# Interleaving the first attention segment with the linear branch's key and value chunks, with early weights aliased into late feature storage

## The chip, the cores and the metric

The kernel runs on one core of one Trainium2 chip. The metric is the device time of one execution in microseconds (us); the time given for a kernel is the median of its runs. Besides the timed runs there is one profiled execution, whose span runs from its first to its last instruction.

## What is computed

Two attention branches read the same x (2048 rows, width 640, 32 heads of 20), and a sigmoid gate per row mixes them. Branch A is linear attention with softmax feature maps. Branch B cuts the rows into four segments of 512; within a segment it is softmax attention under a causal mask, and a memory carried from segment to segment is mixed in per head.

```python
# A: linear attention
pq, pk = q @ w_phi, k @ w_phi                      # per head, 20 x 20
phi_q = concat(softmax(pq), softmax(-pq)); phi_k = likewise
kv = phi_k^T v;  z = sum_s phi_k                   # over all 2048 rows
a  = ((phi_q kv) / (phi_q z + 1e-6)) @ A_wo
# B: four segments, M = z = 0 before the first
p = softmax(qs ks^T * 20**-0.5 + mask)
o = g * (phi(qs) M / (phi(qs) z + 1e-6)) + (1 - g) * (p vs)
M, z = M + phi(ks)^T vs, z + sum phi(ks)           # phi(t) = t+1 if t>0 else exp(t)
b = o @ B_wo
out = gate * a + (1 - gate) * b                    # gate = sigmoid(x . gate_w)
```

## The kernel before

x is held transposed in SBUF (`xT`, 5 chunks of 128 features by 2048 rows), in quarters loaded by transposing DMAs. PSUM is used as four single banks (`bank`, tag "one") and two double banks (`banks2`, tag "two"). The double banks serve folded weights, key features and attention scores alike.

The program runs in stages, in this order.

1. *Fold.* Key weights are transposed on TensorE (`transposed`, from `WkN` to `WkT`) and multiplied by the feature matrix `Wphi` (`fold_weight`), giving `WkA`.
2. *Linear keys and values.* For each of sixteen chunks of 128 rows, `key` multiplies by `WkA`, takes two exponentials on ScalarE (`Ek`), and on VectorE sums them per head, inverts and multiplies (`ksum`, `krec`, `phk`). `value` multiplies by `WvA` and ScalarE copies the result to `vA`. From chunk 8 on, the query weights are folded into `WqA`, and from chunk 10 on ScalarE permutes the columns of `stq` into `WqB` (L272). The instructions here are mostly placed by the framework's scheduler.
3. *Query projection of segment 0, sums and products.* Five `emit_q` run among 160 tiny matmuls that sum the features (`zb_ps`). VectorE adds them in 32 small steps (L321), and `kv_ps` forms the products (L333).
4. *Gates and pools.* The gates of rows and heads are computed for all rows at once, the pools of the first part are closed, and those of the second part opened.
5. *Segment 0's keys and values* (L664 to L671).
6. *The list.* `ORDER` is a string of letters, each one unit of work, that goes out in just that order; matmuls, ScalarE work and some GpSimd work are pinned to it with `keep_in_program_order`. Eighty P's run through it, five for each pair of head groups.

| letter | unit |
|---|---|
| P | one pair of score tiles: matmuls into both double banks, two exponentials `PT` of 128x1024 on ScalarE (L377), causal selects on GpSimd (L547) |
| V, M | a group's values (40 small matmuls, `nd_ps`) and its memory read and update |
| Y | query features of a group for the memory read |
| k, K | half a chunk of B's keys into `kpads` (two buffers), with a transposing DMA to `kTs` after the second half; and its features `phik` |
| v, w | half a chunk of B's values, evicted by VectorE (v) or ScalarE (w) |
| q, u | one fifth of a segment's queries into `qd` (two buffers), evicted by VectorE (q) or ScalarE (u), and scattered into `qTp` by DMAs on SP's queue |
| f, d, n | branch A's query features, weights and outputs |
| l, o, z | loading a row block transposed, and half of its output projection |
| t, b, p | the start of the tail |

After the list comes a tail: the last values and memory read, and the output projections of the last segment.

All weights are loaded on SP's queue: `WkN` and `WvA` first, then `xT` and `WqT` by transposing DMAs, then `WkB`, `WvB`, `stq`, `WoA`, `WoB` (L89 to L162).

Of the kernel before, what the change touches and what calls it, by code (L numbers as in the profile page):

```python
# [7 lines left out]
ACT = mybir.ActivationFunctionType  # L8
# [7 lines left out]
def kernel(  # L16
# [38 lines left out]
    def banks2(name):  # L55
# [12 lines left out]
    wAs = ExitStack()  # L68
    wA = wAs.enter_context(tc.tile_pool(name="wA", bufs=1, side="right"))
# [4 lines left out]
    wA1 = ExitStack()  # L74
    wk = wA1.enter_context(tc.tile_pool(name="wk", bufs=1, side="right"))
    WkA = wk.tile([P, KC, D], BF16, name="WkA")
    WvA = wk.tile([P, KC, D + 1], BF16, name="WvA")
    Wc = wk.tile([P, KC, DH], BF16, name="Wc")
    WkN = wk.tile([P, KC, D], BF16, name="WkN")
    WkT = wk.tile([P, KC, D], BF16, name="WkT")  # L80
    WqT = wk.tile([P, KC, D], BF16, name="WqT")
    nc.scalar.dma_start(out=Wc, in_=A_w_phi.rearrange("h f g -> (h f) g").rearrange("(c p) g -> p c g", p=P))
    nc.scalar.dma_start(out=WvA[:, :, D:D + 1],
                        in_=gate_w.rearrange("(c p o) -> p c o", p=P, o=1))
    beta_b = const.tile([P, H], BF16, name="beta_b")
    nc.scalar.dma_start(out=beta_b, in_=B_beta.partition_broadcast(P))
    def load_xT(lo, hi):
        nc.sync.dma_start_transpose(out=xT[:, :, lo:hi], in_=x2[lo:hi, :])
    nc.sync.dma_start(out=WkN, in_=A_wqkv[:, D:2 * D].rearrange("(c p) n -> p c n", p=P))  # L89
    nc.sync.dma_start(out=WvA[:, :, 0:D],  # L90
                        in_=A_wqkv[:, 2 * D:3 * D].rearrange("(c p) n -> p c n", p=P))
    load_xT(0, P)
    load_xT(P, L)
    for q4 in range(1, 4):
        load_xT(q4 * L, (q4 + 1) * L)
    nc.sync.dma_start_transpose(out=WqT, in_=A_wqkv[:, 0:D])

    NW = 8
    wz = wk.tile([P, L], BF16, name="wz")
    nc.vector.memset(wz, 0.0)
    wu = bank([P, L], "warm_ps")
    for n in range(WARM):
        m = nc.tensor.matmul(wu, lhsT=wz[:, 0:P], rhs=wz, start=True, stop=True)
        if n:
            tc.keep_in_program_order(m)
    ident_f = wk.tile([P, P], F32, name="ident_f")  # L110
    nc.gpsimd.memset(ident_f, 0.0)
    tc.keep_in_program_order(nc.gpsimd.affine_select(
                            out=ident_f, in_=ident_f, pattern=[[-1, P]],
                            compare_op=ALU.not_equal, fill=1.0, base=0,
                            channel_multiplier=1))
    ident = wk.tile([P, P], BF16, name="ident")
    nc.vector.tensor_copy(out=ident, in_=ident_f)
    for t in qTp:
        nc.vector.memset(t, 0.0)
    hn_f = wk.tile([P, KC, NW], F32, name="hn_f")  # L120
    tc.keep_in_program_order(nc.gpsimd.memset(hn_f, 1.0))
    tc.keep_in_program_order(nc.gpsimd.affine_select(
                            out=hn_f, in_=hn_f, pattern=[[8, KC], [-DH, NW]],
                            compare_op=ALU.is_ge, fill=0.0, base=0, channel_multiplier=1))
    tc.keep_in_program_order(nc.gpsimd.affine_select(
                            out=hn_f, in_=hn_f, pattern=[[-8, KC], [DH, NW]],
                            compare_op=ALU.is_ge, fill=0.0, base=DH - 1, channel_multiplier=-1))
    Wphi = wk.tile([P, KC, NW, DH], BF16, name="Wphi")
    tc.keep_in_program_order(nc.vector.tensor_tensor(
        out=Wphi, in0=Wc[:, :, None, :].to_broadcast([P, KC, NW, DH]),  # L130
        in1=hn_f[:, :, :, None].to_broadcast([P, KC, NW, DH]), op=ALU.mult))
    blk = wk.tile([P, KC, NW // 2], F32, name="blk")
    tc.keep_in_program_order(nc.gpsimd.memset(blk, 1.0))
    nc.gpsimd.affine_select(out=blk, in_=blk, pattern=[[8, KC], [-2 * DH, NW // 2]],
                            compare_op=ALU.is_ge, fill=0.0, base=0, channel_multiplier=1)
    nc.gpsimd.affine_select(out=blk, in_=blk, pattern=[[-8, KC], [2 * DH, NW // 2]],
                            compare_op=ALU.is_ge, fill=0.0, base=2 * DH - 1,
                            channel_multiplier=-1)
    bd01 = const.tile([P, 4], F32, name="bd01")
    tc.keep_in_program_order(nc.gpsimd.memset(bd01, 1.0))  # L140
    nc.gpsimd.affine_select(out=bd01, in_=bd01, pattern=[[-32, 4]],
                            compare_op=ALU.is_ge, fill=0.0, base=0,
                            channel_multiplier=1)
    nc.gpsimd.affine_select(out=bd01, in_=bd01, pattern=[[32, 4]],
                            compare_op=ALU.is_ge, fill=0.0, base=31,
                            channel_multiplier=-1)
    for t in (kpads[:, :, :, DH:32], Msb):
        tc.keep_in_program_order(nc.gpsimd.memset(t, 0.0))


# [4 lines left out]
    WoA = wB.tile([P, KC, D], BF16, name="WoA")  # L155
    WoB = wB.tile([P, KC, D], BF16, name="WoB")
    stq = wk.tile([P, KC, D], BF16, name="stq")
    nc.sync.dma_start(out=WkB, in_=B_wk.rearrange("(c p) n -> p c n", p=P))
    nc.sync.dma_start(out=WvB, in_=B_wv.rearrange("(c p) n -> p c n", p=P))
    nc.sync.dma_start(out=stq, in_=B_wq.rearrange("(c p) n -> p c n", p=P))  # L160
    nc.sync.dma_start(out=WoA, in_=A_wo.rearrange("(c p) n -> p c n", p=P))
    nc.sync.dma_start(out=WoB, in_=B_wo.rearrange("(c p) n -> p c n", p=P))  # L162
# [12 lines left out]
    def transposed(ic):  # L175

        tp = ps.tile([P, KC, P], BF16, name="tp_ps", tag="one", bufs=4)
        for c in range(KC):
            tc.keep_in_program_order(nc.tensor.transpose(
                out=tp[:, c, :], in_=WkN[:, ic, c * P:(c + 1) * P], identity=ident))  # L180
        tc.keep_in_program_order((nc.scalar.copy if ic % 2 == 0 else nc.vector.tensor_copy)(
            out=WkT[:, :, ic * P:(ic + 1) * P], in_=tp))

    def fold_weight(dst, WT, ics=range(KC), pinned=False):
        for ic in ics:
            if pinned:
                for n in ((0, 1, 2) if ic == 0 else (ic + 2,) if ic + 2 < KC else ()):
                    transposed(n)
            fp = banks2("fold_ps")
            for n, w in enumerate(WIN):  # L190
                c, lo, hi = w
                bk = lo // 16
                m = nc.tensor.matmul(fp[:, bk, (lo - 16 * bk) * DH:(hi - 16 * bk) * DH],
# [3 lines left out]
                if pinned and n == 0:  # L197
                    tc.keep_in_program_order(m)
# [660 lines left out]
```

## Time and profile before

| | us |
|---|---|
| median of 3 runs | 328.86 (328.55 to 328.91) |
| span of the profiled execution | 326.7 |
| first exponential of a score | 95.21 |
| end of the last exponential of a score | 310.87 |

The profiled execution's own time isn't given apart from its span; the median of the runs lies 2.2 us above it.

| engine | busy us | share of the span | instructions |
|---|---|---|---|
| TensorE (PE) | 306.2 | 94% | 3915 |
| VectorE (DVE) | 237.6 | 73% | 587 |
| ScalarE (ACT) | 256.2 | 78% | 370 |
| GpSimd (POOL) | 167.5 | 51% | 357 |

Busy time counts an instruction from its start to its end; where matmuls overlap in the array, TensorE counts as busy throughout, so its share isn't the share of its peak. PEld is the weight load of TensorE, which overlaps the matmuls. "SPq" and "ACTq" are the DMA-issuing queues of SyncE and ScalarE. In a group's line, "out<-in" names the tiles, then come the shapes and the count, the busy us and the mean ns of one, and the idle time before them with what ended it.

### The profile page before, as it was taken

The page shows a single profiled execution, that of the slowest core. Times are in us where ns is not written, and L with a number is a line of the kernel's source. Part 1 is how long each engine was busy: PE and PEld are TensorE (multiplying, and loading weights), DVE is VectorE, ACT ScalarE, POOL GpSimd, SP SyncE. Part 2 cuts the span into 40 slices and gives each one's busy share as a digit, 9 for nine tenths or more (in the row PEclk, how much of TensorE's full clock was granted, in tenths as well). Part 3 has the DMA queues.
Part 4 walks back from the last instruction along what each step waited for, and adds up shares of the span by engine and source line. Part 5 has one row for each costly group of instructions (what it writes and reads, how often), then busy time and mean ns, then how long its engine had stood idle before and what let it go on. Part 6 is the DMA issues. An engine that isn't in the chain of part 4 may idle for free.

```text
span 326.7 us, 9643 instructions
## 1 busy us (share of the span) xinstructions
PE 306.2 (94%) x3915; PEld 200.6 (61%) x3915; DVE 237.6 (73%) x587; ACT 256.2 (78%) x370; POOL 167.5 (51%) x357
## 2 busy tenths in 40 slices
PE   8899999999898999889999999999999898999994
PEld 4677766698554566555655666566566555666673
DVE  6599997757752577945879999397879956669622
ACT  3677899610479899999999989998888799978811
POOL 4000000002214557987566999675789676668930
PEclk9999999999999999999999999999999999989999
DMA  7999600020232021514121320442303142225252
GB/s 209 175 212 318 220 2 0 25 59 2 64 74 57 20 51 50 74 22 94 34 59 46 72 57 23 53 97 50 90 22 68 42 64 63 62 62 69 48 108 80
DMA packets 63147, 24.50 MB, mean 75 GB/s; under 512 B 54016, under 2 KB 63104, under 8 KB 63104
## 3 DMA queue, kind: packets, MB, share of 16 engines
q1 hardware_dynamic: 61360, 23.54, 32.1%
q8 instruction: 30, 0.49, 0.6%
q10 hardware_dynamic: 1744, 0.36, 0.5%
q14 instruction: 13, 0.11, 0.1%
HBM read 5.77 MB, written 2.62 MB: 26 GB/s over the span
## 4 chain that ended last, share of the span: by engine, by line
PE 59%; DVE 15%; ACT 11%; POOL 9%; issue 3%; DMA 2%; ACTq 0%; DVEq 0%
PE o_ps L374 10%; PE proj L374 7%; ACT PT L377 7%; PE nd_ps L374 7%; PE q_ps L280 6%; PE k_ps L229 6%; PE st_ps L374 6%; PE v_ps L217 6%; PE pf_ps L374 5%; POOL PT L547 4%; POOL oA L471 3%; DVE t L466 2%; PE kv_ps L333 2%; DMA Wc<-in_A_w_phi_dram 2%; PE mem_ps L374 1%
## 5 line engine op out<-in xcount | busy, mean ns | idle before, releaser
L377 ACT ACTIVATE PT<-st_ps 128x1024 bf16<-128x1024 f32 x160 | 155.8, 1037 | 11.2 <-PE st_ps L374 9.3
L547 POOL TENSOR_SCALAR_AFFINE_SELECT PT<-PT 128x256 bf16<-128x256 bf16 (+1 forms) x224 | 96.4, 450 | 55.7 <-ACT PT L377 54.1
L374 PE MATMUL st_ps<-qTp,kTs 32*128 32x384 bf16 (+3 forms) x512 | 41.7, 301 | 6.3 <-ACT PT L377 6.2
L374 PEld LDWEIGHTS <-PT 128*128 128x128 bf16 x1280 | 36.3, 96 | 7.3 <-issue 2.7
L374 PE MATMUL nd_ps<-vB,PT 128*128 128x32 bf16 x1280 | 39.3, 177 | 1.3 <-POOL PT L547 0.6
L390 POOL MEMSET vB<- 128x16 bf16 x4 | 0.5, 116 | 75.3 <-PE kv_ps L333 75.3
L374 PEld LDWEIGHTS <-xT 128*128 128x128 bf16 x320 | 28.8, 97 | 16.4 <-issue 5.7
L374 PEld LDWEIGHTS <-kTs 32*128 32x128 bf16 (+1 forms) x552 | 16.6, 92 | 32.1 <-issue 27.1
L466 DVE TENSOR_TENSOR t<-num_ps,dd 128x320 f32<-128x320 f32 x64 | 29.0, 481 | 4.6 <-PE num_ps L374 3.8
L471 POOL TENSOR_TENSOR oA<-t,t 128x320 bf16<-128x320 f32 x32 | 27.7, 867 | 4.2 <-DVE t L466 4.0
L374 PEld LDWEIGHTS <-oT 128*128 128x128 bf16 x240 | 22.5, 99 | 11.2 <-issue 2.1
L236 ACT ACTIVATE Ek<-k_ps 128x640 bf16<-128x640 f32 x32 | 21.8, 768 | 8.2 <-ACT vA L222 4.7
L374 PE MATMUL proj<-WvB,xT 128*128 128x320 bf16 x160 | 27.2, 299 | 0.3 <-ACT vB L380 0.3
L374 PE MATMUL proj<-WkB,xT 128*128 128x320 bf16 x160 | 26.4, 299 | 1.2 <-DVE kpads L485 0.6
L241 DVE TENSOR_REDUCE ksum<-Ek 128x64 f32<-128x1280 bf16 x16 | 23.7, 1480 | 5.0 <-ACT Ek L236 5.0
L618 POOL TENSOR_TENSOR oB<-td,tm 128x320 bf16<-128x320 f32 (+2 forms) x25 | 22.0, 881 | 8.0 <-DVE tm L609 8.0
L229 PE MATMUL k_ps<-WkA,xT 128*128 128x320 bf16 x160 | 24.3, 299 | 1.6 <-ACT Ek L236 1.3
L280 PE MATMUL q_ps<-xT,WqB 128*128 128x512 bf16 x100 | 25.3, 380 | 0.2 <-DVE mtmp L623 0.2
L374 PE MATMUL pf_ps<-xT,WqA 128*128 128x512 bf16 x100 | 24.8, 380 | 0.0
L217 PE MATMUL v_ps<-WvA,xT 128*128 128x320 bf16 (+1 forms) x160 | 24.5, 300 | 0.0
L485 DVE CAST kpads<-proj 128x320 bf16<-128x320 f32 x32 | 15.3, 484 | 9.9 <-PE proj L374 9.8
L577 DVE RECIPROCAL rden<-nd_ps 128x16 f32<-128x16 f32 x32 | 8.0, 250 | 20.0 <-PE nd_ps L374 19.7
(114 smaller groups left out, 533.7 us busy)
## 6 DMA issues: line engine op xcount, KB each, us to landing
out_dram<-osb SPq DMA_DIRECT2D x12, 160.0 KB
qTp<-qd SPq DMA_DIRECT2D x8, 128.0 KB
WkN<-in_A_wqkv_dram SPq DMA_DIRECT2D x1, 800.0 KB
WvA<-in_A_wqkv_dram SPq DMA_DIRECT2D x1, 800.0 KB
WkB<-in_B_wk_dram SPq DMA_DIRECT2D x1, 800.0 KB
WvB<-in_B_wv_dram SPq DMA_DIRECT2D x1, 800.0 KB
stq<-in_B_wq_dram SPq DMA_DIRECT2D x1, 800.0 KB
WoA<-in_A_wo_dram SPq DMA_DIRECT2D x1, 800.0 KB
```

Source lines behind the costliest of these rows:

```text
L217: m = nc.tensor.matmul(vp[:, 0:n], lhsT=xT[:, c, sc * P:(sc + 1) * P], rhs=WvA[:, c, half * 320:half * 320 + n], start=(c == 0), stop=(c = ...
L229: m = nc.tensor.matmul(kp[:, half, 0:320], lhsT=xT[:, c, sc * P:(sc + 1) * P], rhs=WkA[:, c, half * 320:(half + 1) * 320], start=(c == 0), ...
L236: nc.scalar.activation(out=Ek[:, sgn, :].rearrange("p (a n) -> p a n", a=2), in_=kp[:, :, 0:320], func=ACT.Exp, scale=1.0 if sgn == 0 else ...
L241: nc.vector.tensor_reduce(out=ksum, in_=Ekv.rearrange("p b f i -> p b i f"), axis=AX.X, op=ALU.add)
L280: nc.tensor.matmul(q_ps, lhsT=WqB[:, cc, c * P:(c + 1) * P], rhs=xT[:, cc, s * L:(s + 1) * L], start=(cc == 0), stop=(cc == KC - 1))
L374: return kept(nc.tensor.matmul(*a, **k))
L377: return kept(nc.scalar.activation(**k))
L466: nc.vector.tensor_tensor(out=tt, in0=nm.rearrange("p (h d) -> p h d", d=DH), in1=Lin.cs[:, t, sgn, 16 * bk_:16 * bk_ + 16, None].to_broad ...
L471: tc.keep_in_program_order(nc.gpsimd.tensor_tensor(out=seg.oA[:, t, bk_ * 320:(bk_ + 1) * 320], in0=ts_[0].rearrange("p h d -> p (h d)"), ...
L485: nc.vector.tensor_copy(out=kp[:, half * 16:(half + 1) * 16, 0:DH], in_=pp.rearrange("p (h d) -> p h d", d=DH))
L547: nc.gpsimd.affine_select(out=v, in_=v, pattern=[[0, n], [1, P]], compare_op=ALU.is_ge, fill=0.0, base=0, channel_multiplier=-1)
L618: tc.keep_in_program_order(nc.gpsimd.tensor_tensor(out=o[:, :, at:at + n1 - n0], in0=td2[:, :, n0:n1], in1=tm2[:, :, n0:n1], op=ALU.add))
```

## The change

Segment 0's projections go first. The fold, the linear keys and values, the sums and products become letters of the list too, and the first attention segment's scores run among them. The list is written anew as one string.

| new letter | unit |
|---|---|
| A, B | `key` and `value` of one chunk of the linear branch |
| S, X | the feature sums of one sign, one product |
| T, F, W | a transposition, a fold into `WkA`, a fold into `WqA` |
| L, D, E | a quarter of `xT`, `WqT`, the rest of the loads |
| I, H, J, G | `Wphi`, the masks, the head gate, the row gate of one segment |
| Z | zeroing of `qTp[1]` |
| R | `second_half`: closes the first part's pools, opens the second's, loads `WoA` and `WoB` |

The letters k, K, v, w, q, u and f now count from segment 0.

```diff
-    nc.sync.dma_start(out=WkN, in_=A_wqkv[:, D:2 * D].rearrange("(c p) n -> p c n", p=P))
-    nc.sync.dma_start(out=WvA[:, :, 0:D],
-                        in_=A_wqkv[:, 2 * D:3 * D].rearrange("(c p) n -> p c n", p=P))
...
+    late = phk.rearrange("p c s n -> p (c s n)")[:, 16 * D:32 * D]
+    WkN = late[:, 0:KC * D].rearrange("p (c n) -> p c n", c=KC)
+    WkT = late[:, KC * D:2 * KC * D].rearrange("p (c n) -> p c n", c=KC)
+    Wphi = late[:, 2 * KC * D:2 * KC * D + KC * 8 * DH].rearrange("p (c h g) -> p c h g", c=KC, g=DH)
+    stq = vA[:, 5:10, :]
+    WqT = vA[:, 10:15, :]
+    wz = vA[:, 15, 0:L]
+    WkA = qTp[1].rearrange("p g l -> p (g l)")[:, 0:KC * D].rearrange("p (c n) -> p c n", c=KC)
...
+    load_xT(0, P)
+    load_xT(P, L)
+    for out_, in_ in ((WkB, rows5(B_wk)),
+                      (WkN, rows5(A_wqkv[:, D:2 * D])),
+                      (Wc, rows5(A_w_phi.rearrange("h f g -> (h f) g"))),
+                      (WvB, rows5(B_wv)),
+                      (stq, rows5(B_wq))):
+        kept(nc.scalar.dma_start(out=out_, in_=in_))
...
+    for c in range(KC):
+        kept(nc.gpsimd.tensor_copy(out=WqB[:, c, :].rearrange("p (r g) -> p r g", g=G),
+                                   in_=stq[:, c, :].rearrange("p (g r) -> p r g", g=G)))
...
-            tc.keep_in_program_order(nc.scalar.copy(
-                out=WqB[:, c, :].rearrange("p (r g) -> p r g", g=G),
-                in_=stq[:, c, :].rearrange("p (g r) -> p r g", g=G)))
...
+    def sums(sgn):
+        zb_ps = bank([P, KC, 4 * NCH], "zb_ps")
...
+    def products(n):
+        c, sgn = divmod(n, 2)
+        kv_ps = bank([P, NW, DH], "kv_ps")
...
+    def second_half():
+        a1.close()
...
+        nc.sync.dma_start(out=lt.WoA, in_=rows5(A_wo))
+        nc.sync.dma_start(out=lt.WoB, in_=rows5(B_wo))
...
-    for c in range(4):
-        for half in range(2):
-            emit_k(seg, c, half)
-            emit_v(seg, c, half, scopy)
-        emit_phik(seg, c)
-        if c in (1, 3):
-            lin_features(0, c // 2)
...
+        "kkkkKkkKkkIKKLETTvTFvTFwTFvFwFvuuwvuHJuuLDLABBAA PB PBGAAB PBAWVAB PMBWAWB "
+        "PBAAWVAWB PBAAMB PBAAB PBAVZM P PS PSXXV PXGXMXX PXXXXRG PVGMk Pqq PkV PMqk PuKku "
+        "PVKkkKkk PKMwwYwV Pvvv PMvkfv PfkKf PVkfYYMf Pkkdk PVKYk PvkM PKqK PnVn PMnYlq PVn "
+        "PMYzn Pznq PnvVn PfMf PluvVv PMof PYfwq PVofv PYMdw PlwVYlz PzMYzkn Pzn PknV "
+        "PMnYlkkK PVMKn PYkun Pkon PnV PMKff PVok PYqfM PYlkfYu PvVMlfz PoKd PwV PMuz "
+        "PvYnlwo PVun PMnwYz PVnwM Pno PvnvnY PVn PlMYfo PVf PMff Pofl PYVMd Pz PlnVM PYYzn "
+        "Pon PnV PMnYlz PnVnM PbYz Pnz PV PMpt ")
```

So the early weights share storage with what is written late: `WkN`, `WkT` and `Wphi` lie in the last eight chunks of `phk`, `stq` and `WqT` in chunks 5 to 14 of `vA`, and `WkA` in the query buffer of segments 1 and 3, which Z zeroes after the last A. The five first weights are issued on ScalarE's queue, the transposing DMAs stay on SP's. Two pools hold the segments (`bseg0`, `bseg1`), the second opened at R, and outputs of branch A and weights of the output projection get storage at R. All ScalarE and TensorE work is now pinned to the list.

## Prediction

> **What bounds the kernel now.** First the busy time by stretch. The columns are the stretch (us), its length, then for each engine the busy us and the instructions, the granted clock, and the DMA share and rate.
>
> ```profile
> 0.00:11.50 11.50, 8.76 (x69) 5.04 (x70) 7.78 (x13) 5.41 (x9) 3.48 (x17) 1.00 0.85 203
> 11.50:58.50 47.00, 45.69 (x351) 33.04 (x351) 41.51 (x62) 38.80 (x76) 0.00 (x0) 1.00 0.58 148
> 58.50:80.00 21.50, 21.30 (x349) 17.75 (x348) 14.42 (x57) 5.75 (x12) 0.12 (x2) 1.00 0.12 33
> 80.00:95.20 15.20, 14.27 (x99) 9.04 (x97) 10.57 (x23) 7.79 (x16) 3.80 (x5) 1.00 0.31 70
> 95.20:203.00 107.80, 101.62 (x1465) 61.76 (x1463) 79.37 (x207) 100.83 (x131) 78.00 (x168) 1.00 0.23 51
> 203.00:311.00 108.00, 103.04 (x1474) 65.64 (x1471) 80.43 (x217) 95.84 (x125) 79.72 (x164) 0.98 0.32 61
> 311.00:326.70 15.70, 11.55 (x121) 8.29 (x118) 3.51 (x11) 1.80 (x5) 2.39 (x4) 0.96 0.35 89
> ```
>
> The 80 score steps fill 95.2 to 311, with ACT busy 196.7 of 215.8 us. From 58.5 to 95.2 ACT has 13.5 of 36.7 us of work, and POOL none before 80. So the exponentials come in one dense block behind a stretch that has almost none. PE looks full everywhere, but its matmuls overlap in the records. The chain that ended last has the true pace (start us, us, what):
>
> ```profile
> 11.52 1.52 PE k_ps L229 x10
> 13.03 1.37 PE v_ps L217 x10
> 67.09 0.99 PE zb_ps L312 x40
> 74.07 5.71 PE kv_ps L333 x80
> 93.12 1.09 PE pf_ps L374 x5
> 104.66 1.01 PE nd_ps L374 x40
> ```
>
> That is 0.137 us for a 320-column matmul (299 ns in the groups), 0.22 for 512 columns and 0.025 for the smallest. At these paces all of PE's work is about 266 us: 80% of the score stage, but about 97% of 11.5 to 58.5 (16 chunks of 2.73 and five folds, 45.5 of 47.0). So PE sets the first stage, closely followed by DVE, and ACT the second. The costliest groups give prices (busy over count):
>
> ```profile
> L377 ACT ACTIVATE PT<-st_ps 128x1024 bf16<-128x1024 f32 x160 | 155.8, 1037 | 11.2 <-PE st_ps L374 9.3
> L236 ACT ACTIVATE Ek<-k_ps 128x640 bf16<-128x640 f32 x32 | 21.8, 768 | 8.2 <-ACT vA L222 4.7
> L241 DVE TENSOR_REDUCE ksum<-Ek 128x64 f32<-128x1280 bf16 x16 | 23.7, 1480 | 5.0 <-ACT Ek L236 5.0
> ```
>
> One P, two exponentials, costs ACT 1.95 us. A key chunk A costs ACT 1.36, PE 1.36 and DVE 2.86 (1.48 + 0.55 + 0.83).
>
> **The method and its test.** For each five P with what the list puts between them I add up each engine's work and take the largest. For before the sixteen maxima are 13.8, 11.9, 12.0, 13.0, 14.4, 14.8, 13.0, 14.0, 14.2, 15.3, 11.8, 14.3, 13.3, 14.4, 12.3 and 11.5, together 214.0; the stage took 215.8, a factor of 1.008. ACT is the largest in most. The factor is so near 1 because the prices carry some slack (an exponential that follows another starts 0.92 us after it, not 0.97).
>
> **The change, part by part.**
>
> *Start to first score.* Removed from the head: WkA's fold as the first work. Added: eight k, six to eight v and five q before any A. The first k needs WkB and xT. WkB is now the first weight in its queue, as WkN was before, which released PE at 6.06, so k starts near 6.3. Eight k take 8 x 0.68 = 5.4. Each pair sends a kTs transpose (SP busy 1.23 us, plus landing), and the two kpads buffers let chunk 2 be evicted only when chunk 0's transpose has landed: about 2 us late. Five T, five F and six v are 7.3 us of PE, and the copies between them are the chain that before took from 6.07 to 12.3. That puts q at about 22.
>
> The q need all of WqB. Its source is the fifth weight; 3.3 MB and 0.65 MB of xT at 209 to 318 GB/s (the page's slices) land at 14 to 20. Then POOL makes five strided copies that ACT made in 1.65 each. The trace has no such copy on POOL: from below by the 128x768 memset, 0.74 x 640/768 = 0.6; from above by the 128x84 cast, 0.27 x 640/84 = 2.1. I take 1.3, nearer the middle because the cast is mostly fixed cost: 6.5 us in all, so q starts at 22 to 27, I take 22.5. Five q then go at the pace of their DMAs:
>
> ```profile
> ACT qd L284 <- DMA qTp<-qd: 5.4, 3, 2.0
> ```
>
> Two qd buffers made ACT wait up to 2.0 us; before, the first eviction to the last took 8.7 us (60.72 to 69.42). Before, PE ran sums meanwhile. Now ACT's queue behind the waiting eviction is Ek of the first A, and DVE and the first P wait for that. Then three A and two B precede the first PT: 3 x 1.36 + 4 x 0.42 = 5.8 of ACT. Sum: 22.5 + 1.5 + 8.7 + 0.6 + 5.8 = 39. Ends: 36 if the q DMAs hide behind the copies, 46 if POOL's copies cost 2.1 and kTs lands late in the weight traffic.
>
> *First 15 P (segment 0's attention among A, B, W, S, X).* Added to the A/B stretch: 30 exponentials (29.2 us of ACT), 42 selects on POOL. Per engine (PE, ACT, DVE): P0-P4 28.2, 33.3, 27.0; P5-P9 18.0, 20.7, 18.6; P10 to the point R 14.9, 6.0, 12.6; R to P14 4.4, 4.3, 4.3. Maxima 33.3 + 20.7 + 14.9 + 4.4 = 73.3, times 1.008 = 73.9; I take 73, since before's 11.5 to 58.5 ran PE and DVE both about full with no slip. W (1.0 of ACT each) is in it; WqB's 8.2 us have left ACT. The sums S and the 32 adds behind them (5.9 of DVE) lie under X. Ends: 68 (PE alone 65.5 plus 4%) and 80 (sum plus 10%).
>
> *The other 65 P.* Maxima 16.0, 17.4, 15.3, 13.6, 16.2, 13.9, 13.3, 16.2, 14.4, 13.3, 15.3, 12.8, 11.3 = 189.0, times 1.008 = 190.5. Four stretches now have PE at the top or beside ACT (16.2 to 15.9, 13.9 to 13.8, 16.2 to 16.1, 16.4 to 17.4), and PE's price has no slack in it. Before's stretch with all engines equal (P50, 11.8) took 14.2. I add 2.5: 193, with ends 185 and 203.
>
> *Moved at no cost.* WoA and WoB are loaded at R: SP's queue holds their issue until the last X, and behind it wait the q of segment 1; the first output projection comes some eighteen P later. xT's later quarters and WqT are issued behind the kTs and qTp DMAs, and W0 needs WqT some 10 us after its issue; without that cover W0 holds both fold and key buffers for about 5. The late aliases are reused only after their last reader in the list. The zeroing of qTp[1] (1.76 of DVE) lies in P7, where DVE has 5 against ACT's 4. Evictions shift slightly: 13 instead of 19 vB and 12 instead of 8 qd on ACT, less than 1 us net.
>
> *Tail:* the same work, 15.7.
>
> **Sum:** 39 + 73 + 193 + 15.7 = 320.7, against the profiled 326.7. The median of the runs, 328.86, lies 2.2 above the span, so 322.9; I say **322.5**.
>
> **A rule against it.** DVE's phk multiply (both inputs in SBUF) never ran beside POOL: it took 824 to 826 ns. The like operation that does run beside POOL is spread wide:
>
> ```profile
> L526 DVE TENSOR_TENSOR phiq<-uq,eq x24: 411/678/1083, 137.5 to 298.3; 128x512 bf16<-128x512 bf16 x24
> ```
>
> Thirteen phk will now run beside selects, so by this row each loses 0.27 (median over minimum) to 0.67 us (maximum over minimum): 3.5 to 8.7 in all. The Trainium skill, SBUF — State Buffer, "Who interferes with whom", says that VectorE and GpSimd take a shared port pair by an exclusive lock for a whole instruction; the spread agrees with it, though it doesn't prove it. P0-P9 have DVE at 45.6 against ACT's 54.0, so 8.4 us of cover: I add nothing, and it is a rival.
>
> **The rivals.**
>
> 1. *Two-bank chain* (slower). Key chunks, folds and scores share two double banks. PE can't fill an A until an exponential has drained one, and 1.36 us of filling is longer than one exponential (0.97). If ACT idles for a whole fill at each of thirteen A, 13 x 1.36 = 17.7: 340. It decides the sign from 6.4/13 = 0.5 us each. For it: ACT's longest idle in the first stage, Ek waiting for k_ps (2.8 us over 3 times). Against: B's evictions lie between, and in before's score stage PE waited only 6.2 us for ACT in 80 P.
>
> 2. *Late start.* The first PT at 47 instead of 39 (WqB late, q DMAs unhidden): 330.5, no gain. For it: q's wait above; against: the DMA was idle from 41 to 57, so weights aren't short of bandwidth.
>
> 3. *Port lock decides.* All of 8.7 on the path: 331. Against: the cover.
>
> 4. *Better packed.* First 15 P at 68, the rest at 185, start at 37: 305.7 span, 308. For it: before's first stage ran PE near 97%. Against: ACT held only 91% over before's score stage.
>
> 5. *It doesn't interleave.* The built instruction order has A and B among the scores on PE and ACT, and the same 3915 matmuls; I leave it out.
>
> **How the numbers follow.** Chances: forecast 0.52 (own range 315 to 328), two-bank chain 0.18, late start 0.10, port lock 0.06, better packed 0.14. Faster by over 0.2% (what a measurement here can tell): 0.50 + 0.14 + 0.04 from an incomplete late start = 0.68; within 0.2%: 0.03; slower 0.29. The range 311 to 337 leaves out the lower part of the packed case and the upper end of the chain.
>
> **What would show it.** First PT near 39 (36 to 46); P15's PT near 112; the last PT near 305; the tail at 15.7. ACT idle in 39 to 95 under 10% with the releaser not k_ps. The wait of qd for qTp near 5 us. phk's spread above 826 ns but DVE not ahead of ACT in P0-P9. It would be wrong if ACT is idle over 6 us on k_ps in P0-P8, if the first PT comes after 46, or if the 65 later P take more than 200.

## The result, and the profile after

The changed kernel took 340.76 us (median of 4 runs, 338.86 to 342.15), beside 328.88 us (328.55 to 329.03) for the kernel before on the same chip: a ratio of 1.0365, with a 95% interval of 1.032 to 1.0409. The forecast was 322.5 with a range of 311 to 337, so both the sign and the range were wrong. The profiled execution has a span of 337.1 us (its run took 338.86), where the forecast's sum was 320.7. One run of the experiments' last batch, 340.25 us, stood 1.9% above the fastest of its kernel and is left out there.

Busy time by stretch, cut at the first and every later P that the forecast's terms name (columns as in the prediction's table: stretch, length, then busy us and instructions of PE, PEld, DVE, ACT and POOL, the granted clock, and the DMA's share and rate):

```profile
0.00:47.06 47.06, 34.63 (x226) 20.98 (x227) 24.10 (x48) 17.59 (x32) 12.16 (x25) 0.93 0.67 167
47.06:79.11 32.05, 31.24 (x319) 21.29 (x319) 26.08 (x45) 29.36 (x56) 8.61 (x16) 1.00 0.26 47
79.11:101.23 22.12, 20.62 (x264) 14.12 (x264) 20.10 (x33) 19.33 (x31) 8.44 (x16) 0.91 0.01 2
101.23:123.81 22.58, 22.58 (x376) 19.40 (x376) 14.87 (x67) 9.97 (x14) 9.48 (x24) 0.87 0.18 58
123.81:220.54 96.73, 93.31 (x1257) 59.03 (x1257) 72.57 (x196) 83.22 (x114) 62.51 (x131) 0.98 0.36 68
220.54:321.60 101.06, 96.59 (x1379) 61.95 (x1378) 74.11 (x203) 89.33 (x119) 76.51 (x149) 0.97 0.35 59
321.60:337.10 15.50, 11.19 (x104) 8.03 (x104) 3.52 (x11) 1.60 (x4) 2.45 (x4) 0.96 0.30 80
```

The first three rows after the head are P0 to P4, P5 to P9 and P10 to P14. Set against the sum:

| term | forecast | measured | over by |
|---|---|---|---|
| first P starts | 39 | 47.06 | 8.1 |
| first 15 P | 73 | 76.75 | 3.75 |
| other 65 P | 193 | 197.8 | 4.8 |
| tail | 15.7 | 15.5 | -0.2 |
| span | 320.7 | 337.1 | 16.4 |

The head isn't that steady. Four later kernels leave it as it is here and change only what follows; in their profiles the first P stood at 49.77, 48.77, 48.85 and 48.55. So 47.06 is an early one, and a shift of the first P by less than some 2.7 us in a single profile tells nothing.

Two observations stand in these rows. ACT, which held 91% of the score stage before, holds 231.2 of 274.5 us now, 84%. And the clock column isn't 1.00: in the score stage the granted clock is at half from 97.0 to 107.2 and for 3.4 us each at 168.7, 291.6 and 305.3, 20.5 us in all. The kernel before had 3.4 us of it there. The changed kernel's four runs had a mean clock of 0.954 to 0.970, the kernel before 0.993 in its profile.

The costliest exponentials, and what ACT waited for from the first P to 124 us and from there to 322 us (us in total, times, longest):

```profile
L108 ACT ACTIVATE PT<-st_ps 128x1024 bf16<-128x1024 f32 x160 | 156.2, 1039 | 32.7 <-PE st_ps L105 29.8
```

```profile
ACT PT L108 <- PE st_ps L105: 14.0, 6, 5.8
...
ACT Ek L108 <- PE k_ps L105: 0.2, 1, 0.2
```

```profile
ACT PT L108 <- PE st_ps L105: 16.4, 26, 1.6
```

The exponential costs the same as before (1039 against 1037 ns), but ACT now waits 29.8 us in front of it for the scores, where it waited 9.3. The key features (Ek) hardly wait for the matmul engine: 0.2 us.

The head, on the matmul engine, on POOL and on DVE (start us, us, engine, line, operation, count, and in brackets the idle time before and what ended it):

```profile
7.24 1.53 PE L105 MATMUL proj<-WkB,xT 128*128 128x320 bf16 x10 [1.02 <-DMA xT<-in_A_x_dram]
14.52 6.20 PE L105 MATMUL proj<-WkB,xT 128*128 128x320 bf16 x30 [5.74 <-DMA xT<-in_A_x_dram]
23.00 0.84 PE L194 MATMUL tp_ps<-ident,phk 128*128 128x128 bf16 x10 [2.29 <-DVE kpads L477]
```

```profile
15.02 6.95 POOL L176 COPY WqB<-vA 128x640 bf16<-128x640 bf16 x5 [8.86 <-DMA vA<-in_B_wq_dram]
```

```profile
16.07 0.49 DVE L477 CAST kpads<-proj 128x320 bf16<-128x320 f32 x1 [6.41 <-PE proj L105]
16.48 1.39 DVE L150 CAST ident<-ident_f 128x128 bf16<-128x128 f32 x1
...
18.38 0.95 DVE L491 TENSOR_SCALAR uk<-kpads 128x640 bf16<-128x640 bf16 x1
19.25 1.41 DVE L256 TENSOR_TENSOR hm<-blk,par 128x40 bf16<-128x40 f32 x1
```

Only two of the eight k ran near 7 us (five matmuls each). The other six waited until 14.52 for the second piece of xT, which shared the DMA engines with weights not needed yet: from 9 to 13 us they moved some 245 packets of 256 bytes per us for xT and some 240 of 1280 bytes for the weights, one for one, so 0.06 MB per us for what was waited for and 0.31 for what was not. Then POOL's five copies (1.39 us each) held DVE's small operations: the cast of the identity took 1.39 us here and 0.21 where POOL was idle (shown in the first experiment). The queries started at 31.72 instead of 22.5.

### The profile page after: what moved, and what is told of

The parts are those of the page before. It is cut to its first block, busy times and chain, and to the rows that moved or that the text cites. A ratio compares the mean times of both kernels' runs of the same rounds, so it can differ in the third digit from the quotient of the medians.

```text
span 337.1 us, 9662 instructions
## 1 busy us (share of the span) xinstructions
PE 310.2 (92%) x3915; PEld 204.8 (61%) x3915; DVE 235.3 (70%) x598; ACT 250.4 (74%) x367; POOL 180.2 (53%) x362
## 4 chain that ended last, share of the span: by engine, by line
PE 50%; DVE 11%; ACT 10%; POOL 5%; issue 4%; ACTq 0%; DVEq 0%
PE o_ps L105 9%; PE proj L105 6%; PE nd_ps L105 6%; PE st_ps L105 5%; ACT PT L108 5%; PE q_ps L105 4%; PE pf_ps L105 4%; PE kv_ps L105 4%; PE k_ps L105 3%; POOL PT L539 3%; PE v_ps L105 3%; PE mem_ps L105 2%; ACT ET L108 2%; PE num_ps L105 2%; ACT WqA L111 1%
## 5 line engine op out<-in xcount | busy, mean ns | idle before, releaser
L108 ACT ACTIVATE PT<-st_ps 128x1024 bf16<-128x1024 f32 x160 | 156.2, 1039 | 32.7 <-PE st_ps L105 29.8
L539 POOL TENSOR_SCALAR_AFFINE_SELECT PT<-PT 128x256 bf16<-128x256 bf16 (+1 forms) x224 | 100.4, 467 | 114.4 <-ACT PT L108 112.3
L105 PEld LDWEIGHTS <-xT 128*128 128x128 bf16 x640 | 60.1, 99 | 37.8 <-DMA xT<-in_A_x_dram 7.6
L105 PEld LDWEIGHTS <-kTs 32*128 32x128 bf16 (+1 forms) x552 | 15.8, 92 | 30.6 <-issue 25.8
L105 PE MATMUL proj<-WkB,xT 128*128 128x320 bf16 x160 | 27.2, 316 | 6.9 <-DMA xT<-in_A_x_dram 6.8
L105 PE MATMUL proj<-WvB,xT 128*128 128x320 bf16 x160 | 26.4, 299 | 1.0 <-DVE mtmp L615 0.6
L477 DVE CAST kpads<-proj 128x320 bf16<-128x320 f32 x32 | 15.0, 480 | 15.9 <-PE proj L105 15.9
L105 PE MATMUL q_ps<-xT,WqB 128*128 128x512 bf16 x100 | 24.4, 382 | 0.4 <-DVE kpads L477 0.4
L105 PE MATMUL k_ps<-qTp,xT 128*128 128x320 bf16 x160 | 23.5, 299 | 0.2
L108 ACT ACTIVATE ET<-pf_ps 128x512 bf16<-128x512 f32 x40 | 21.9, 634 | 2.4 <-PE pf_ps L105 2.4
L108 ACT ACTIVATE Ek<-k_ps 128x640 bf16<-128x640 f32 x32 | 20.8, 706 | 3.3 <-ACT WqA L111 1.9
L105 PE MATMUL o_ps<-WoA,oT 128*128 128x320 bf16 x120 | 21.6, 313 | 0.3 <-DVE t L458 0.3
```

Of the source, the lines that this page charges most:

```text
L105: return kept(nc.tensor.matmul(*a, **k))
L108: return kept(nc.scalar.activation(**k))
L477: nc.vector.tensor_copy(out=kp[:, half * 16:(half + 1) * 16, 0:DH], in_=pp.rearrange("p (h d) -> p h d", d=DH))
L539: nc.gpsimd.affine_select(out=v, in_=v, pattern=[[0, n], [1, P]], compare_op=ALU.is_ge, fill=0.0, base=0, channel_multiplier=-1)
```

## The experiments

The first batch took the head and the clock one by one and together; the second combined what the first had taught; the third measured what an extra us of one engine costs; the last asked whether the head and the uneven stretches can be mended. The kernel before had medians of 328.56, 328.59, 328.43 and 328.22 us beside them.

### x first

The four weights after WkB are issued behind a tiny copy on ACT's queue that waits for xT's second piece.

```diff
+    kept(nc.scalar.dma_start(out=WkB, in_=rows5(B_wk)))
+    landed = const.tile([P, 1], BF16, name="landed")
+    scopy(out=landed, in_=xT[:, 0, L - 1:L])
+    for out_, in_ in ((WkN, rows5(A_wqkv[:, D:2 * D])),
...
```

> The changed kernel, but on ScalarE's queue only WkB is issued at once; the four other early weights (WkN, Wc, WvB, stq) wait until the second piece of xT has landed. Theory (queues share by packets: xT's 256-byte packets got 240 per us beside 240 of the weights' 1280-byte packets, and the third k waited for xT until 14.52): the third k starts near 9, TensorE's clock doesn't fall at 11.7 to 18.5, the first PT comes at 38 to 41 instead of 47.06, and the time falls by 5 to 8 us to 333 to 336. Rival (the start is set by the lock between GpSimd's WqB copies and VectorE, or by the q DMAs): the third k comes early all the same, but the first PT stays within 2 us of 47 and the time at 339 to 342.

Measured 345.0 us, ratio 1.0517 (1.0454 to 1.058). The k ran from 7.00 to 12.6 us, as the theory said, but the first P came at 52.2, later than before. DVE in that head:

```profile
9.73 0.21 DVE L152 CAST ident<-ident_f 128x128 bf16<-128x128 f32 x1
...
17.62 0.89 DVE L479 CAST kpads<-proj 128x320 bf16<-128x320 f32 x2 [5.82 <-DMA kTs<-kpads]
...
21.62 0.89 DVE L479 CAST kpads<-proj 128x320 bf16<-128x320 f32 x2 [2.71 <-DMA kTs<-kpads]
...
23.59 3.00 DVE L493 TENSOR_SCALAR uk<-kpads 128x640 bf16<-128x640 bf16 x2
26.51 3.33 DVE L496 TENSOR_TENSOR phik<-uk,ek 128x640 bf16<-128x640 bf16 x2
```

The delayed weights now share the DMA engines with the transposes into kTs, so the evictions wait for those (8.5 us in two waits), and the copies on POOL, now from 21.40 to 29.48, hold uk and phik. The waiting had moved, not gone. The P stretches were as in the changed kernel (32.05, 22.13, 22.66 and 16.90 against 32.05, 22.12, 22.57 and 17.07, and 197.7 against 197.8 for the last 65 P): a later head shifts the rest and nothing else.

### Masks early

The identity, mask and head-mask copies are pinned early on DVE, and so are segment 0's evictions into kpads.

```diff
-        nc.vector.tensor_copy(out=kp[:, half * 16:(half + 1) * 16, 0:DH],
-                              in_=pp.rearrange("p (h d) -> p h d", d=DH))
+        first(nc.vector.tensor_copy(out=kp[:, half * 16:(half + 1) * 16, 0:DH],
+                              in_=pp.rearrange("p (h d) -> p h d", d=DH)), seg.s)
```

> The changed kernel, but VectorE's identity, masks and their copies are pinned ahead of the first evictions of k, so that they don't run while GpSimd permutes WqB (15.02 to 21.97, in which these small steps took 1.2 to 1.4 us each instead of 0.16 to 0.28). Theory (the lock with GpSimd delays the kpads evictions): the fifth k is evicted near 18.5 instead of 22.47, the first PT comes 3 to 4 us earlier, and the time falls by 3 to 4. Rival (the eviction waits for the kTs transpose anyway): first PT within 1 us of 47.06 and no change of time.

Measured 339.95 us, ratio 1.0351 (1.0324 to 1.0378), first P at 47.6: no gain. Another operation meets POOL's copies in their place:

```profile
18.45 2.75 DVE L491 TENSOR_SCALAR uk<-kpads 128x640 bf16<-128x640 bf16 x2
21.12 1.45 DVE L292 CAST CM<-bd 128x32 bf16<-128x32 f32 x1
```

### Sums mixed with products

Each S also issues two of the products X, so that matmuls of 4 and of 160 columns alternate.

```diff
+            for sg, kv_ps in enumerate(kvs):
+                mm(kv_ps, lhsT=phk[:, sc, sg, sgn * P:(sgn + 1) * P],
+                   rhs=vA[:, sc, 6 * sgn * DH:(6 * sgn + NW) * DH],
+                   start=(sc == 0), stop=(sc == NCH - 1))
```

> The changed kernel, but each of the two sums S is issued with two of the products X between its matmuls (4 or 5 narrow ones, then 2 of 160 columns); the same matmuls in all. Theory (narrow matmuls alone let the granted clock fall to half at 97.0 to 107.3): the clock stays full there, or falls for 3.4 us at most, the ten P from P5 to P15 take 41 to 42 instead of 44.7 us, and the time falls by 2 to 4. Rival (the stretch is set by VectorE's phk, which is late by then): the same clock or not, P5 to P15 takes 44 to 45 and the time stays.

Measured 347.55 us, ratio 1.0574 (1.0546 to 1.0602). The clock got worse: at half for 17.1 us instead of 10.2, and P5 to P15 took 48.7 us instead of 44.7. The theory in this form falls. (2.7 of the 6.8 us that this run is slower stand in the head, which the edit leaves alone.)

```profile
101.30:118.40 17.10, 16.27 (x285) 15.38 (x285) 5.66 (x24) 4.48 (x6) 3.62 (x9) 0.50 0.01 3
```

So mixing wider matmuls into the sums doesn't keep the clock. The stretch just ahead is the next place to look, here in the changed kernel's PE between 94 and 97 us:

```profile
93.83 1.17 PE L105 MATMUL nd_ps<-vB,PT 128*128 128x32 bf16 x40
94.85 0.31 PE L105 MATMUL mem_ps<-vB,phik 128*128 128x84 bf16 x4
95.09 0.73 PE L105 MATMUL st_ps<-qTp,kTs 32*128 32x512 bf16 x4
96.59 0.34 PE L105 MATMUL st_ps<-qTp,kTs 32*128 32x384 bf16 x2 [0.78 <-ACT PT L108]
```

Small matmuls, scores on 32 rows, and a wait.

### All three

> The three edits together: four weights wait for xT, masks early, sums mixed with products. Theory (start and clock are the causes): first PT at 37 to 40, P5 to P15 in 41 to 42, time 328 to 332, that is within 1% of the kernel before. Rival (what is gained at the head is lost to waits further on, since the later scores are bound by themselves): first PT early, but the time stays above 335.

Measured 352.02 us, ratio 1.0709 (1.0677 to 1.0742), first P at 53.8, P5 to P15 48.6: each part did about what it had done alone.

### Projections in the sparse stages

Three of segment 1's query projections move into the stretch just named, one behind the scores of each of three P's, ahead of the sums there.

```diff
-        "PBAAWVAWB PBAAMB PBAAB PBAVZM P PS PSXXV PXGXMXX PXXXXRG PVGMk Pqq PkV PMqk PuKku "
+        "PBAAWVAWB PBAAMB PBAAB PBAVZM Pu PuS PuSXXV PXGXMXX PXXXXRG PVGMk P PkV PMk PuKku "
```

> Edit: three of segment 1's query projections are moved from the P stages around 110 to 130 us into the three sparse P stages just before them (94 to 98 us in the changed kernel's profile), where the matmul engine has little but narrow score matmuls to do; nothing else changes. Theory (the granted clock falls to half at 97.0 to 107.3 us because the stages just before it have too few columns to stream): with some 9000 more columns there the clock stays full, the stretch from P5 to P15 falls from 44.7 to about 42 us although 3.2 us of work is moved into it, P15 to P20 falls from 17.1 to about 15.5, and the time falls by 3 to 5 us to 336 to 338. Rival (the fall has nothing to do with how dense these three stages are, or comes with the sums that follow): the half clock stays within 95 to 110 us, P5 to P15 grows to 47 or 48, and the time stays at 340 to 342.

Measured 338.64 us (338.18 to 340.45), ratio 1.0317 (1.028 to 1.0354). The half clock at the sums is gone. First the changed kernel, then this one, at about the same place (the first P is 1.7 us later here):

```profile
94.00:97.00 3.00, 2.16 (x50) 1.30 (x47) 2.62 (x4) 2.78 (x4) 0.70 (x2) 1.00 0.00 0
97.00:107.20 10.20, 9.54 (x200) 8.60 (x200) 6.81 (x21) 4.34 (x5) 3.88 (x10) 0.50 0.01 3
```

```profile
99.00:109.20 10.20, 9.99 (x247) 8.35 (x247) 6.33 (x21) 5.47 (x8) 3.87 (x9) 1.00 0.16 42
```

So the clock fell because the work of these P's was too thin: with 3.2 us of projections more it stays full through the very same sums. All four profiles with these projections have no half clock there (each has 3.4 us of it some 25 us later), all nine profiles of the changed kernel and its variants without them have 6.8 to 17.1 us. The projections stand ahead of the sums and between them, so this run doesn't tell the two places apart; a count at the end of this text does, and both were too thin. The time is another matter: P5 to P15 took 43.2 us with one projection more in it on balance (1.1 us), 2.6 less than expected from 44.7, but the later 3.4 us of half clock stand at 124.0, and P15 to P20 took 17.9 instead of 17.1. The theory's cause of the half clock is shown, and its 3 to 5 us are not: the two ratios' intervals overlap.

### Masks early and four padded buffers

The masks as above, and segment 0's third and fourth key chunk get padded buffers of their own, so that no eviction waits for the transposes of the first two.

```diff
+    kpads2 = vA.rearrange("p c n -> p (c n)")[:, 0:64 * 32].rearrange(
+        "p (b h e) -> p b h e", b=2, e=32)
...
-        kp = kpads[:, c % 2]
+        kp = kpads[:, c % 2] if seg.s or c < 2 else kpads2[:, c - 2]
```

> Edit: the identity, mask and head-mask copies stand early on VectorE, and segment 0's third and fourth key chunk get padded buffers of their own, so that no eviction waits for the transposes that read the first two. Theory (first P at 47.06 rather than 39 because the eviction of the fifth key half waited for a transpose that shares the queues with the weights, so that the key transposes on the matmul engine started at 23.0): these start at 18 to 19, the first P at 43 to 44, and the time falls by 3 to 4 us to 337. Rival (the copies of the query weight on POOL, 1.39 us each from 15 to 22 us, hold VectorE's small operations anyway): the first P stays at 46 to 48 and the time at 339 to 341.

Measured 339.43 us (337.4 to 341.01), ratio 1.0327 (1.0284 to 1.037): the rival, which had 339 to 341. The first P stood at 46.5. The buffers were free, but the last six k still began at 14.70, and uk and CM still met POOL's copies.

### The head mended, without and with the projections

All of the head's edits at once (x first, masks early, four buffers), and the five WqB copies as a letter Q, in turns on DVE and ACT, none on POOL.

```diff
+        elif kind == "Q":
+            kept((nc.scalar.copy if n % 2 else nc.vector.tensor_copy)(
+                out=WqB[:, n, :].rearrange("p (r g) -> p r g", g=G),
+                in_=stq[:, n, :].rearrange("p (g r) -> p r g", g=G)))
```

> Edit: all head edits together: four weights wait for the second piece of x on ScalarE's queue, masks early, four padded buffers, and the query weight's five copies are on VectorE and ScalarE in turns, none on POOL. Theory (the 8.1 us at the head are three delays in a row: x shares the queues with weights that are not needed yet, the evictions wait for transposes, and the copies on POOL hold VectorE): key projections 7 to 12.6 us, first P at 37 to 41, time 331 to 335. Rival (transposes collide with the delayed weights, as they did when x alone was put first): first P at 46 or later and the time at 339 or more.

> Edit: the mended head and the three query projections in the sparse P stages together. If both theories hold and their gains add up: 327 to 331 us, within 1% of the kernel before. If the head's gain is real but the clock falls elsewhere: 331 to 335. If neither: 340.

Measured 335.89 us (334.07 to 336.31), ratio 1.0212 (1.0181 to 1.0242), without the projections, and 333.55 us (333.13 to 336.54), ratio 1.0171 (1.0125 to 1.0216), with them. The first is between theory and rival, the second in its middle case. The mended head:

```profile
13.11 0.73 PE L195 MATMUL tp_ps<-ident,phk 128*128 128x128 bf16 x10 [0.92 <-DMA phk<-in_A_wqkv_dram]
18.67 1.51 PE L105 MATMUL proj<-WvB,xT 128*128 128x320 bf16 x5 [4.83 <-DMA WvB<-in_B_wv_dram]
```

The transposes ahead of the fold begin at 13.11 instead of 23.00, 9.9 us earlier, but the first P stands at 44.9, only 2.2 earlier. The value weight is late now, and behind it stand the copies of the query weight: the queries start at 27.19 instead of 31.72. The run with the projections has the same head, and there they start at 24.99 and the first P stands at 42.55. So the three delays were real, and they covered a fourth; what the mended head is worth lies between 2.2 and 7.2 us by these profiles (42.55 and 44.9 against 47.06 to 49.77).

### One engine's price

What does an extra us cost? One more 512-column matmul ahead of each P's scores, whose product the scores overwrite, or one more 128x64 copy on ACT behind each P; both in the changed kernel and in the kernel before.

```diff
+        kT, qT = parts[0][2], parts[0][3]
+        mm(st[0][:, 0, 0:L], lhsT=kT[:, 0:P], rhs=qT[:, 0:L], start=True, stop=True)
```

```diff
+        dum = bpt.tile([P, 64], BF16, name="dum", bufs=1)
+        scopy(out=dum, in_=parts[0][2][:, 0:64])
```

> Edit: the changed kernel with one more 512-column matmul at the front of each of the 80 P (its product is overwritten by the scores, nothing else changes): 80 x 0.216 = 17.3 us more for the matmul engine, nothing for the others. Theory (the matmul engine's own order sets the pace of the whole score stage; the forecast took 266 us for its work, where the spacing of the matmul starts gives some 283): the time grows by 14 to 18 us, to 355 to 359. Rival (as the forecast had it, ScalarE sets the pace in most of the last 65 P and the matmul engine has a fifth of spare time): it grows by at most 8.

> Edit: the changed kernel with one more small ScalarE copy (128 x 64) behind each of the 80 P: 80 x about 0.2 = 16 us more for ScalarE, nothing for the others. Theory (matmul engine sets the pace): the time grows by 2 to 6 us. Rival (ScalarE sets it): by 11 to 16 us.

> Edit: the same extra matmul in the kernel before. Theory (there too the matmul engine is near its limit, with some 29 us not streaming in the score stage of 216): the time grows by 8 to 14 us. Rival (ScalarE sets that stage, as the forecast read it, with the matmul engine at four fifths): by at most 4.

> Edit: the same extra ScalarE copy in the kernel before. Theory (both engines near their limits, ScalarE busy 91% of the score stage): the time grows by 4 to 10 us. Rival (ScalarE alone sets it): by 12 to 16.

| | time, us | over its own kernel | ratio to before |
|---|---|---|---|
| changed, extra matmul | 346.02 | +5.3 | 1.053 (1.0498 to 1.0562) |
| changed, extra copy | 340.59 | -0.2 | 1.0361 (1.0324 to 1.0399) |
| before, extra matmul | 337.39 | +9.0 | 1.0268 (1.0237 to 1.0298) |
| before, extra copy | 329.73 | +1.3 | 1.0046 (1.0024 to 1.0069) |

The groups of the extra copy, in the changed kernel and in the kernel before:

```profile
L111 ACT COPY dum<-kTs 128x64 bf16<-128x64 bf16 x80 | 21.3, 266 | 0.0
```

```profile
L380 ACT COPY dum<-kTs 128x64 bf16<-128x64 bf16 x80 | 22.0, 275 | 0.0
```

The next instruction on ACT starts 0.13 us after a copy's start, so the 80 take 10.7 us of ACT, not the 16 of the expectation. Of these the kernel before pays 1.3, and the changed kernel nothing that can be told (its own interval is 1.5 us to either side). The matmul's 17.3 us cost 9.0 and 5.3. So ACT sets the pace of neither score stage, and PE is nearer to it without setting it alone. Of the eight expected ranges two were met: 9.0 lies in the theory's 8 to 14 for the kernel before, and 5.3 within the rival's bound of 8 for the changed kernel, where the theory had 14 to 18. Both copies came out below theory and rival. Part of the 5.3 is the clock: with the extra columns the profiled score stage had 6.8 us at half clock instead of 20.5, and the mean clock of the four runs was 0.975 to 0.980 instead of 0.954 to 0.970, so the extra matmuls repaid something of their price.

### The head's order, and an evener filling

On top of the mended head with the projections: the second quarter of x (L) and the linear branch's value weight (E) are issued behind the WqB copies, and four transposes and the first two folds stand ahead of the first value half. Then, in a second kernel, two f and the d move from P20 to P25 into P25 to P30 as well.

```diff
-        "kkkkKkkKkkIKKLETTvTFvTFQwTFQvFQwFQvQuuwvuHJuuLDLABBAA PB PBGAAB PBAWVAB PMBWAWB "
+        "kkkkKkkKkkIKKTTTFTFvTFQwFQvFQwQvQEuuLwvuHJuvuLDLABBAA PB PBGAAB PBAWVAB PMBWAWB "
```

```diff
-        "PVKkkKkk PKMwwYwV Pvvv PMvkfv PfkKf PVkfYYMf Pkkdk PVKYk PvkM PKqK PnVn PMnYlq PVn "
+        "PVKkkKkk PKMwwYwV Pvvv PMvkfv PfkKf PVkYYM Pkkk PVKYkf PvkMf PKdqK PnVn PMnYlq PVn "
```

> Edit: on top of the mended head with the three query projections, the second quarter of x and the linear branch's value weight are issued behind the five query weight copies rather than ahead of the folds, and the transposes and first fold stand ahead of segment 0's first value half. Theory (the mended head is still late because the value and query weights land behind transfers that are not needed yet): the wait of 2.9 to 4.8 us for the value weight goes, queries start at 21 to 23 rather than 25 to 27, the first P stands at 38 to 40, the time is 329 to 331. Rival (the queries are late for another cause, the copies or the transfers of the queries themselves): the first P stays at 42 to 45, the time at 333 to 336.

> Edit: the same, and two of branch A's query features and the weights formed from them move from the stretch P20 to P25, where the matmul engine is full (16.8 us of work in 17.6), to P25 to P30 (10.2 us of work in 14.8). Theory (uneven filling is what the later 65 P lose): P20 to P25 shrinks by about 2 us to 15.5, P25 to P30 grows by less than 0.5, time 1.5 to 2 us below the run without it. Rival (waits and not the filling set these stretches): the sum of the two stretches stays at 32.4.

Measured 335.0 us (333.82 to 335.25), ratio 1.0189 (1.0163 to 1.0216), and 337.1 us (334.19 to 338.94), ratio 1.0281 (1.0247 to 1.0315). Neither is a gain over 333.55. In the first, the queries started at 24.95 rather than 21 to 23, as early as without the new order (24.99), and the first P came at 44.1. ACT from 10 to 47 us:

```profile
ACT qd L111 <- DMA qTp<-qd: 7.4, 3, 4.3
```

L now lies between the query transfers on SP's queue, and the fifth query waits 4.3 us for them: the rival's second cause. In the second kernel, whose head has the same order, the first P came at 40.4: between two profiled executions the head differs by some 4 us. Its stretch P20 to P25 fell to 15.5 us as expected, but P25 to P30 rose from 14.8 to 20.5. What PE waited for there, and the clock (columns as above):

```profile
PE num_ps L105 <- DVE td L576: 2.2, 1, 2.2
```

```profile
149.40:163.50 14.10, 11.73 (x187) 7.26 (x188) 10.46 (x29) 11.98 (x16) 8.19 (x19) 1.00 0.33 66
163.50:169.90 6.40, 4.89 (x36) 2.36 (x38) 6.30 (x18) 2.46 (x3) 3.50 (x7) 0.50 0.02 4
```

The weights (d) now stand just ahead of the outputs that need them, with DVE's reciprocals between. PE waits for them: it was busy for 1.96 of the 3.40 us ahead of 163.5, and for the next 6.8 us the clock is at half (36 matmuls in the 6.4 us shown). In this form the theory of uneven filling gained nothing; whether a filling that leaves d its lead would, wasn't tried.

## Why the prediction was wrong

Two steps failed, and each alone is worth more than the 6.0 us that the forecast's sum lay below the profile of before: the start of the first P (8.1) and the pace of the 80 P (3.75 + 4.8). Of the prediction's three signs of being wrong one came, a first P after 46.

**A count of PE's work.** Take each matmul to last until the next one's start, but at most the spacing of its kind in an unbroken run: 0.025 us for up to 32 columns, 0.056 for 128, 0.069 for 160, 0.136 for 320 and 0.216 for 512. The scores need a term more. They use 32 of the array's 128 rows, and four of them start within 0.01 us. When PE passes from other matmuls to scores, the next start comes 0.096 us later than the spacing (0.232 after 320 columns, 0.312 after 512), and on the way back 0.09 to 0.10 later (0.147 after 128 columns, 0.316 after 512); I count this as work. What's left of the span is time in which PE streams nothing or streams at half clock:

| us | head | score stage | tail | whole |
|---|---|---|---|---|
| before: work | 85.9 | 192.7 | 11.3 | 289.9 |
| before: rest | 9.3 | 23.0 | 4.5 | 36.7 |
| after: work | 29.5 | 247.9 | 10.8 | 288.3 |
| after: rest | 17.6 | 26.6 | 4.7 | 48.8 |

This is worked out from the trace's starts, and gaps smaller than a spacing count as work. Without the term for the scores the work is 274.0 and 273.3 us; the rest then grows by 11.2 instead of 12.1, so the level depends on the count and the growth hardly does.

**"PE's work is about 266 us: 80% of the score stage", and so "ACT the second", was the step that failed for the pace.** By this count the work of the kernel before is 289.9, 24 us more, and it filled 89% of the score stage (192.7 of 215.7). Of the 24, 15.9 are the 84 passages into the scores and out again, for which the prediction names no price; the extra copies refute that ACT sets that stage: 10.7 us more of ACT cost 1.3. A change that moves PE's work between stages without lessening it can win only from the rest. The forecast's span of 320.7 left 32.4 us of it, 18.1 in a score stage with 55 us more to do. The kernel got 26.6 there, and 17.6 in the head where the forecast left 9.5. Against the kernel before, the rest grew by 8.3 in the head and 3.6 in the score stage, where the changed kernel also has 20.5 us at half clock.

**First P at 39: wrong by 8.1,** the largest single term. "That puts q at about 22" failed: they started at 31.72. The step let eight k run without a break as soon as WkB and xT's first piece were there; it didn't ask in what order two queues are served. Of the 9.2 us by which q was late, PE waited 5.74 for xT's second piece and 2.29 for the evictions into kpads. From q to the first P took 15.3 where 16.5 was forecast, and the q's wait for their DMAs was 5.2 us ("near 5"). POOL's copies were 1.39 each (1.3 forecast), but their price lay elsewhere, in DVE's operations beside them. The Trainium skill, DMA: Bandwidth & Descriptors, "Queues, rings and completion order", says that a DMA engine takes its queues in turns, a packet (several descriptors) at a time; the one-for-one counts above agree with turns of equal length.

**First 15 P at 73: over by 3.75.** P0 to P4 took 32.05 against 33.3, P5 to P9 22.12 against 20.7, P10 to P14 22.58 against 19.3. Ten us at half clock fall in the last two, a term that the forecast put at nothing. That 32 products (kv_ps) took 4.28 us at half clock and 2.39 at full accounts for 1.9 us.

**The other 65 at 193: over by 4.8.** In the run with four padded buffers, whose profile shows no half clock there, they took 196.8, so the clock explains about 1 and some 4 are left. "A factor of 1.008" was calibrated on stretches that each had slack on PE as it was priced; that waits between the engines come on top where PE is full would explain the 4, but no run shows it. With the 39 us head that was forecast and the other terms as measured, the span would have been 329.0: still no gain over 326.7.

**Tail and moved loads:** as forecast, 15.5 and no wait seen.

**The rivals.** The two-bank chain falls: Ek waited 0.2 us for k_ps where 17.7 were its price. Late start came true in its place (47; measured 47.06), but its size is luck: its two causes were a late WqB and unhidden query DMAs, and WqB was ready at 21.97 and the query DMAs cost the 5.2 us that the forecast held anyway, while xT and the evictions were late. It explains half of the miss. Port lock in P0 to P9 falls: phk ran at 760 to 1250 ns with the median still at 824, and P0 to P4 were faster than forecast. It acted in the head, where I hadn't priced it. The Trainium skill, SBUF — State Buffer, "Who interferes with whom", gives the loser a wait for a whole instruction; the 1.39 us of the cast beside copies of 1.39 agree with it. Better packed falls with its premise: "PE near 97%" was a full stage, which leaves nothing to gain. That the clock would fall was in no rival.

**What stays open.** No version beat the kernel before; the best stands at 1.0171 (1.0125 to 1.0216). How much of the score stage's 26.6 us could be had with another list isn't shown, nor what sets the pace there in each wait: PE's work is the largest term, and no engine's alone accounts for the time.

## What to carry to other kernels

Before moving work to fill idle engines, count the time in which the busiest one streams nothing, from the spacing of its starts rather than from its busy share, and include what it costs to change from one kind of matmul to another: what is left is all that a reordering can win. And price an engine by adding to it: 80 small copies showed in one run that the engine that looked like the bound wasn't. When work is brought to the front, list what shares its DMA engines, since each delay taken away here uncovered the next.

## What the runs showed of the hardware

- The granted clock fell to half while PE was shown as busy for 2.16 of 3.00 us. In the changed kernel the stretch from 93.8 to 97 us has only values of 32 columns, four matmuls of 84 and six scores, with one wait of 0.78 us, and the next 10.2 us are at 0.50; with three projections more the clock stayed at 1.00 through the same sums. With matmuls of 4 and 160 columns mixed it stayed down for 17.1 us. Half-clock stretches that end inside the span came as 3.4, 6.8, 10.2 and 17.1 us, multiples of 3.4. The Trainium skill, TensorE: Matmul & The Clock Gate, "What's actually happening", tells of a window of about 3.4 us over which busyness is watched; the lengths agree, and here 72% of busy time in small matmuls was not enough.
- What PE streams tells where the clock falls, and its busy time much less. Cut the score stages of the sixteen traces into windows of 3.41 us on the grid of the half-clock stretches, and count in each the columns of the matmuls that start in it, those of a score by a quarter, since it uses 32 of the 128 rows. Of the 36 windows after which the clock fell, 35 have under 3060 such columns (some 8100 would fit at 0.216 us for 512), and of the 1131 after which it stayed full only 6; at half clock it stayed down after all 21 windows under 3060 and came back after all 36 above. The windows after which it fell were busy for 46% to 92%; by busy time the best line misplaces 29 of the windows at full clock, by these columns 7. In the changed kernel the windows from 93.6 on have 2640, 632, 1640 and 4160; with the three projections the same place has 5120, 3392 and 3424; with sums and products mixed it has 1088, then 2380 to 3056 four times, then 3572. The line is fitted to these traces, and a score's weight isn't settled: a half, with another line, fits as well.
- Passing from matmuls over 128 rows to scores over 32, and back, cost PE about 0.1 us each way beyond the spacing (0.232 instead of 0.136 after 320 columns; 0.316 instead of 0.216 after a score of 512), some 15 us in 80 P.
- Two DMA queues shared one for one by the trace's packets: 245 of 256 bytes against 240 of 1280 in the same us, so the queue with small packets had a sixth of the bytes.
- A 128x64 copy on ACT shows 0.27 us but lets the next instruction start after 0.13: its busy time is twice what it takes from the engine.
